# Attention and two feed-forward layers on one core: a new order of the first words (query transposes, row sums, values, weight conversion)

## The chip, the cores and the metric

The kernel runs on one core of one Trainium2 chip. The metric is device time in microseconds (us) of one launch, the median of several runs: 1700.97 us before (three runs, 1700.34 to 1705.41). Engines are named as in the profile: PE (matrix multiply), PEld (its weight loads), DVE (VectorE), ACT (ScalarE), POOL (GpSimd) and SP, whose queue issues most transfers.

## The reference, cut to what matters

```python
B, H, S, D = 8, 8, 576, 64                      # pool = 8, so Sp = 72
k_p = k.reshape(B, H, Sp, 8, D).mean(axis=3)    # v_p the same of v
scores = (1 / sqrt(D)) * q @ k_p.T
attn = exp(scores - scores.max(-1))
attn = attn / (attn.sum(-1) + 1e-9)
x = (attn @ v_p)  # to [4608, 512]
x = (relu(x @ w_in) ** 2) @ w_out               # 512 -> 2048 -> 512
out = leaky(x @ w2_in, 0.01) @ w2_out           # the same sizes
```

The weights come in as 64-bit numbers, two 32-bit words each, and are made into sums of two rounded 32-bit parts (a high and a low one) on the chip.

## The kernel before, in words

The 4608 tokens go in blocks of 512, four tiles of 128 tokens each. The beginning, which the change is about, does four things at once: attention for the four tiles of block 0, then, between the products of the first layer, attention for block 1 (tiles 4 to 7), and all the while the conversion of the first layer's weights, eight pieces of w_in and eight of w_out.

The order is written out by hand. A string, `START`, holds words of a letter and a number; `start()` (line 749) goes through them and issues each word's instructions, and every engine then takes its own in that order, each waiting for its operands. The words:

- `K`, `Q`, `V`, `i`: the loads of keys, of a query tile, of values, of a weight piece (all on SP's queue).
- `k`: pools the keys (DVE, line 429), masks them (446), transposes them on PE (460) and copies them with ACT (464).
- `q`: transposes a query tile on PE (562), and ACT copies it out (567).
- `s`: the scores of a tile on PE (598); for each half DVE takes the maximum (610, "m" below) and ACT four exponentials (619), eight a tile.
- `n`: the row sums (DVE, 630, only where the tile's number is in `early`), their reciprocals and the scaling (631 to 633), and a copy of the last columns (640).
- `P`: the transposes of the probabilities on PE (661, 667) and ACT's two casts (671, 673); `r`: DVE's low parts of them (680).
- `v`: pools the values, matmuls on PE (392) and two sums on DVE (402); `m`: splits them (DVE, 526 to 541); `w`: ACT places them (524, six instructions); `x1`: the key pooling of batch 1 on PE (392).
- `a` to `e` of a weight piece: `a` one ACT pass (231), `b` two DVE passes (235, 238), `c` two (249, 252), `d` one (293), then a cast by ACT (298, `D` on its own) and `e`, one more on DVE (302). In the string before, the word `d` stands for both `d` and the cast.

Behind `start()` come the values of block 0 (PE, lines 712 to 715, with a cast by ACT and a subtraction by DVE for each of four groups), and `first_products()`: 32 units of 12 matmuls each (line 883), the pieces of tiles 4 to 7 and of the conversion hung into them by `second_attention()` and `conversion(u)`. Then `second_products()` (line 921) and the remaining blocks.

PSUM has eight banks: four with the names acc0 to acc3 and four that `bank()` hands out in turn (`ps`). `acc_bank(m)` takes one by name. A new user of a bank waits until the last reader of it is done.

Of the kernel before, what the change touches and what calls it, by code (L numbers as in the profile page):

```python
# [12 lines left out]
AF = mybir.ActivationFunctionType  # L13
ALU = mybir.AluOpType
AX = mybir.AxisListType

P = 128
# [26 lines left out]
def attention_relu2_leaky_kernel(  # L44
# [12 lines left out]
    nc = tc.nc  # L57
    B, H, S, D = q.shape
# [4 lines left out]
    NP = H // 2  # L63
    KEYS = H * SP
    NK = (KEYS + P - 1) // P
    KC = DM // P
    FC = DFF // P
    RD = POOL * D
    RROWS = 6 * REM
    T = 512  # L70
    BLOCKS = NT // T

    START = (
        "K0 Q0 i0 Q1 Q2 Q3 V0 i1 K1 i2 Q4 Q5 i3 "
        "q0 k0 a0 s0 q1 b0 s1 q2 c0 n0 s2 q3 n1 s3 P0 d0 n2 r0 P1 n3 r1 a1 v0 P2 r2 m0 P3 r3 w0 e0 x1"
    ).split()

    common = ctx.enter_context(tc.tile_pool(name="sb", bufs=1, side="left"))
# [64 lines left out]
    def drop(what, b, n):  # L146
        for c in range(n):
            taken((what, b, c))
# [13 lines left out]
    def taken(key):  # L162
        tag = raws.pop(key)[1]
        if tag:
            live[tag] -= 1
            load()
# [58 lines left out]
            for j in range(2)  # L225
        ]

    def exponent(top):


        nc.scalar.activation(out=f32(top), in_=f32(top), func=AF.Copy, scale=2.0**-112)

    def first_bits(val, top):

# [9 lines left out]
            op1=ALU.bitwise_or,  # L244
        )

    def low_term(val, top, low):

        nc.vector.tensor_scalar(
            out=top, in0=val, scalar1=0xFF800000, scalar2=None, op0=ALU.bitwise_and  # L250
        )
        nc.vector.scalar_tensor_tensor(
            out=f32(low),
            in0=low,
            scalar=2.0**-52,
            in1=f32(top),
            op0=ALU.mult,
            op1=ALU.mult,
        )

    def place(kind, i, t):
        for n, to in enumerate(((wih, wil), (woh, wol))[kind]):
# [10 lines left out]
    def weight_steps(w, kind, i):  # L273


        st = {}

        def load_words():
            t = sb([P, 1024, 2], U32, weight_tag(kind, i))
            src, to = words_of(w, kind, i)  # L280
            nc.sync.dma_start(out=to(t), in_=src)
            st["low"], st["top"] = t[:, :, 0], t[:, :, 1]

        def bits():
            val = st["val"] = sb([P, 1024], U32, "val")
            first_bits(val, st["top"])

        def term():
            low_term(st["val"], st["top"], st["low"])

        def high():
            w = st["w"] = f32(st["val"])
            nc.vector.tensor_tensor(out=w, in0=w, in1=f32(st["low"]), op=ALU.add)
            t = st["parts"] = sb([P, 2, 1024], F32R, weight_tag(kind, i))
            place(kind, i, t)

        def high_copy():
            nc.scalar.copy(st["parts"][:, 0], st["w"])

        def low():  # L300
            t = st["parts"]
            nc.vector.tensor_tensor(out=t[:, 1], in0=st["w"], in1=f32(t[:, 0]), op=ALU.subtract)

        return load_words, lambda: exponent(st["top"]), bits, term, high, low, high_copy

    class Weights:

# [71 lines left out]
                self.tick()  # L379


    first_tiles, first_s, early = range(T // P), [], range(2 * T // P)
    kps, kts, kms, vps, vrps, vst, qT, sc = {}, {}, {}, {}, {}, {}, {}, {}
    v_hi = sb([P, NP, P], F32R, "v_hi")
    v_lo = sb([P, NP, P], F32R, "v_lo")
# [90 lines left out]
    def v_pool_pe(b):  # L476

        vps[b] = sb([P, NP, D], F32, "vp")
        vrps[b] = sb([P, 2, D], F32, "vr")
        ps, last = acc_bank(2), acc_bank(3)  # L480
        for cc in range(NP):
            halves(ps, cc, raws[("v", b, cc)][0], P)
        for c in range(2):
            halves(last, c, raws[("rem", b, c)][0], RROWS)
        halves_sum(vps[b], ps, 0, NP)
        halves_sum(vrps[b][:RROWS], last, 0, 2)

    def v_tile_pe(b, what, c):

# [85 lines left out]
    def score_products(i):  # L575

        rest = []
        qt = qT.pop(i)
        if i in first_tiles:
            if not first_s:  # L580
                t = home_tile([P, 3, KEYS]).rearrange("p n (h k) -> p n h k", h=H)
                first_s.extend(t[:, n] for n in range(3))
            s = first_s.pop()
        else:
            s = sb([P, H, SP], F32, "s")
        m = sb([P, H], F32, "m")
        l = sb([P, H], F32, "l")
        for hf in range(2):
            if i in first_tiles:
                ps = acc_bank((2 * i + hf) % KC)  # L590
            else:
                ps = acc_bank(KC - 1) if i in early and hf == 0 else bank()
# [145 lines left out]
    def start():  # L738

        t0, rest = 0, {}  # L740
        for word in START:
            x, n = word[0], int(word[1:])
            if x == "K":
                for c in range(NK):
                    if n:
                        load_to(("k", n, c), k_load(n, c), ("gh", "gl", "gh", "gl", "raw")[c])
                    else:
                        load_home(("k", n, c), k_load(n, c))
                keyed.add(n)
            elif x == "Q":  # L750
                load_q(n)
            elif x == "V":
                for c in range(NP):
                    load_home(("v", n, c), v_load(n, c))
                for c in range(2):
                    load_home(("rem", n, c), rem_load(n, c))
                pooled.add(n)
            elif x == "i":
                w1.load(n)
            elif x in "abcde":  # L760
                w1.do("dD" if x == "d" else x, n)
            elif x == "k":
                for c in range(NK):
                    k_pool(n, c)
                k_mask(n)
                k_transpose(n)
                drop("k", n, NK)
            elif x == "x":
                pooled_late.append(k_pool_pe(n))
                drop("k", n, NK)  # L770
            elif x == "v":
                v_pool_pe(n)
                drop("v", n, NP)
                drop("rem", n, 2)
            elif x == "m":
                v_split(n)
            elif x == "w":
                built.add(n)
                v_place(n)
            elif x == "q":  # L780
                q_transpose(n)
                taken(("q", n))
            elif x == "s":
                scores(n)
            elif x == "n":
                normalize(n)
            elif x == "P":
                rest[n] = p_products(n, 0, t0)
            elif x == "r":
                rest.pop(n)()  # L790
# [201 lines left out]
    w1, w2 = Weights(w1_in, w1_out), Stored(w2_in, w2_out)  # L992
# [62 lines left out]
    LATE, LAST = 6, FC - 3  # L1055
    begins = {2 * n - 2 if n < LATE else 2 * LATE + 1 + (n - LATE) * 5 // 2: n for n in range(1, LAST + 1)}

    def conversion(u):
        if u in begins:
            n = begins[u]  # L1060
            if n < LAST and n + 1 != LATE:
                w1.do("a", n + 1)
            w1.do("bcd" if n == 1 else "cdD", n)
        elif u - 1 in begins:
            n = begins[u - 1]
            if n == 1:
                w1.do("D", n)
            if n < LAST and n + 1 != LATE:
                w1.do("b", n + 1)
            if n != LATE - 1:  # L1070
                w1.do("e", n)
        elif u == 2 * LATE:
            w1.do("ab", LATE)
# [581 lines left out]
```

## Time and profile before

| | us |
|---|---|
| median of the runs (three) | 1700.97 |
| the profiled execution, by itself | 1704.66 |
| its span, first to last instruction | 1702.9 |
| PE busy in the span | 1663.1 |
| DVE, ACT busy | 1156.0, 703.9 |

PE is busy 98% of the span, so its idle stretches are where time can come from. The page's 40 slices are 42.6 us each: PE is at 6 tenths in the first one and at 9 everywhere else but the last. A row of the timeline has the start, the length, the engine, line and operation, out and in, and in brackets the engine's idle time before it and what ended that.

### The profile page before, as it was taken

What the parts mean: (1) busy time and instruction counts of PE and PEld (TensorE: products, weight loads), DVE (VectorE), ACT (ScalarE), POOL (GpSimd) and SP (SyncE); (2) the same over time, 40 slices, a digit from 0 to 9 for tenths busy, and PEclk for the clock granted to TensorE, in tenths of its full rate; (3) what the DMA queues carried; (4) which work ended last, traced back from release to release, by engine and by line L of the source; (5) the groups of instructions that cost most, each with busy time, mean ns of one, the idle gap of its engine ahead of it and who ended that gap; (6) DMA issues with size and microseconds to landing.
All of it is one profiled execution on the core that took longest, in us unless ns stands there. A gap on an engine that the chain in (4) does not pass through costs nothing. (4 is left out here: it accounts for less than half of the span.)

```text
span 1702.9 us, 25369 instructions
## 1 busy us (share of the span) xinstructions
PE 1663.1 (98%) x9608; PEld 1500.0 (88%) x9608; DVE 1156.0 (68%) x2028; ACT 703.9 (41%) x1551; POOL 19.6 (1%) x39
## 2 busy tenths in 40 slices
PE   6999999999999999999999999999999999999998
PEld 5778888888888888888888899999999999999998
DVE  7978886666666667575534677756767866666665
ACT  4545343343443443433433444434444633333332
POOL 0012000000000000000000000000000000000000
PEclk9999999999999999999999999999999999999999
DMA  8924542323233232332001255355437755454443
GB/s 229 342 88 156 173 152 94 89 89 96 88 98 98 86 97 74 96 110 73 30 25 56 86 172 177 118 179 174 170 126 257 259 164 164 150 158 155 155 149 106
DMA packets 197211, 228.24 MB, mean 134 GB/s; under 512 B 49120, under 2 KB 157920, under 8 KB 197088
## 3 DMA queue, kind: packets, MB, share of 16 engines
q1 hardware_dynamic: 193952, 217.70, 39.8%
q0 software_dynamic: 2560, 8.39, 1.3%
q8 instruction: 75, 1.23, 0.3%
q10 hardware_dynamic: 576, 0.52, 0.1%
q14 instruction: 48, 0.39, 0.1%
HBM read 140.58 MB, written 85.98 MB: 133 GB/s over the span
## 5 line engine op out<-in xcount | busy, mean ns | idle before, releaser
L883 PE MATMUL ps<-xh,wi 128*128 128x512 f32 x896 | 296.6, 393 | 0.0
L921 PE MATMUL acc<-gh,wo 128*128 128x512 f32 x1080 | 276.6, 394 | 0.7 <-ACT xl L893 0.7
L921 PEld LDWEIGHTS acc<-gh,wo 128*128 128x128 f32 x1080 | 200.7, 189 | 41.7 <-ACT xl L893 1.2
L883 PEld LDWEIGHTS ps<-xh,wi 128*128 128x128 f32 x896 | 168.2, 188 | 34.6 <-issue 0.2
L883 PE MATMUL ps<-xl,wi 128*128 128x512 f32 x448 | 174.4, 389 | 0.0
L900 DVE CAST gh<-r 128x512 fp32r<-128x512 f32 x112 | 47.6, 425 | 175.0 <-ACT r L896 174.6
L893 ACT ACTIVATE r<-ps 128x512 f32<-128x512 f32 x112 | 67.7, 605 | 207.8 <-PE ps L883 203.6
L921 PE MATMUL acc<-gl,wo 128*128 128x512 f32 x540 | 149.5, 390 | 0.0
L921 PEld LDWEIGHTS acc<-gl,wo 128*128 128x128 f32 x540 | 101.8, 189 | 21.6
L619 ACT ACTIVATE s<-ps,m 128x72 f32<-128x72 f32 x240 | 72.1, 330 | 93.4 <-DVE m L610 93.4
L883 PEld LDWEIGHTS ps<-xl,wi 128*128 128x128 f32 x448 | 84.2, 188 | 16.5
L1537 PE MATMUL acc<-wi,hh 128*128 128x256 f32 x512 | 94.0, 283 | 1.1 <-ACT r L1353 1.1
L1537 PE MATMUL acc<-wo,hh 128*128 128x256 f32 x512 | 93.8, 283 | 0.0
L1537 PE MATMUL ps<-wo,hh 128*128 128x256 f32 x496 | 90.9, 283 | 0.0
L1537 PE MATMUL ps<-wi,hh 128*128 128x256 f32 x496 | 90.9, 283 | 0.0
L1337 PE MATMUL acc<-fh,wi 128*128 128x384 f32 x408 | 88.4, 339 | 1.3 <-DVE gh L1350 0.3
L1337 PE MATMUL ps<-fh,wo 128*128 128x384 f32 x408 | 87.7, 337 | 0.0
L901 DVE TENSOR_TENSOR gl<-r,gh 128x512 fp32r<-128x512 f32 x112 | 77.6, 693 | 7.5
L1537 PEld LDWEIGHTS acc<-wi,hh 128*128 128x128 f32 x512 | 79.9, 192 | 1.3 <-ACT r L1353 1.3
L1537 PEld LDWEIGHTS acc<-wo,hh 128*128 128x128 f32 x512 | 79.9, 192 | 0.0
L1353 ACT ACTIVATE gh<-gh 128x384 f32<-128x384 f32 x48 | 25.3, 526 | 131.1 <-DVE gh L1350 131.1
L1537 PEld LDWEIGHTS ps<-wo,hh 128*128 128x128 f32 x496 | 77.4, 192 | 0.0
(278 smaller groups left out, 3560.9 us busy)
## 6 DMA issues: line engine op xcount, KB each, us to landing
hf<-r SPq DMA_DIRECT2D x96, 192.0 KB
xl<-hf SPq DMA_DIRECT2D x24, 640.0 KB
hr<-hf SPq DMA_DIRECT2D x24, 640.0 KB
xh<-hf SPq DMA_DIRECT2D x23, 640.0 KB
hf<-gl SPq DMA_DIRECT2D x48, 192.0 KB
hf<-gh SPq DMA_DIRECT2D x48, 192.0 KB
hf<-st SPq DMA_DIRECT2D x48, 192.0 KB
wi<-in_moe_w_in SPq DMA_DIRECT2D x8, 1024.0 KB
```

The source lines that it names most:

```text
L619: nc.scalar.activation(out=s[:, g, :], in_=ps[:, h * SP : (h + 1) * SP], func=AF.Exp, bias=m[:, g : g + 1], accum_out=None if i in early e ...
L883: nc.tensor.matmul(ps, lhsT=w[:, kc], rhs=x[kc], start=(kc == 0 and n == 0), stop=(kc == KC - 1 and n == 2),)
L893: nc.scalar.activation(out=r, in_=ps, func=AF.Relu)
L900: nc.vector.tensor_copy(gh, r)
L901: nc.vector.tensor_tensor(out=gl, in0=r, in1=f32(gh), op=ALU.subtract)
L921: nc.tensor.matmul(acc[m], lhsT=w[:, m * P : (m + 1) * P], rhs=x, start=(c == 0 and n == 0), stop=(c == FC - 1 and n == 2),)
L1337: nc.tensor.matmul(at, lhsT=w[:, FORMS[j], kc], rhs=x[j][:, kc], start=m == 0 and j not in (4, 6), stop=m == 5, skip_group_check=True,)
L1353: nc.scalar.activation(out=out_, in_=x, func=AF.Lrelu)
L1537: nc.tensor.matmul(at[:, s * TR : (s + 1) * TR], lhsT=x[:, a, s * P : (s + 1) * P], rhs=w[:, b], start=p == 0 and s == 0 and m == 0, stop= ...
```

## The change

- `START` is ordered anew. Query transposes 1, 2 and 3 come one tile ahead of the scores that need the tile before. Query tiles 0 to 2 are loaded ahead of weight piece 0.
- Weight piece 0's `a b c d` come behind the scores of tile 2, together, instead of being spread from the first scores on; its cast `D` and `e` behind the transposes of tile 1. Piece 1's `b c d` are done before the low parts `r1`, not after the first products have begun.
- `early` is empty: in tiles 0 to 7, too, ACT gives the row sums along with the exponentials, and the row-sum instruction of DVE goes.
- The values are pooled in two of the four turning banks instead of acc2 and acc3, on PE behind the scores of tile 3, and their sums on DVE are a word of their own (`u`).
- `conversion(u)` does the pieces 1 to 4 earlier in the first products. The order of later units stays.
- Engines for the conversion can be chosen by `BY_GPSIMD`, which is empty, so nothing goes to GpSimd.

```diff
+    BY_GPSIMD = ()
     START = (
-        "K0 Q0 i0 Q1 Q2 Q3 V0 i1 K1 i2 Q4 Q5 i3 "
-        "q0 k0 a0 s0 q1 b0 s1 q2 c0 n0 s2 q3 n1 s3 P0 d0 n2 r0 P1 n3 r1 a1 v0 P2 r2 m0 P3 r3 w0 e0 x1"
+        "K0 Q0 Q1 Q2 i0 Q3 V0 i1 K1 i2 Q4 Q5 i3 "
+        "q0 k0 q1 s0 q2 s1 n0 q3 s2 a0 b0 c0 d0 n1 P0 s3 v0 r0 n2 P1 D0 a1 e0 "
+        "n3 u0 P2 m0 b1 c1 d1 r1 P3 w0 r2 x1 r3"
...
-    first_tiles, first_s, early = range(T // P), [], range(2 * T // P)
+    first_tiles, first_s, early = range(T // P), [], range(0)
...
-        ps, last = acc_bank(2), acc_bank(3)
+        ps, last = bank(), bank()
...
-        halves_sum(vps[b], ps, 0, NP)
-        halves_sum(vrps[b][:RROWS], last, 0, 2)
+        def rest():
+            halves_sum(vps[b], ps, 0, NP)
+            halves_sum(vrps[b][:RROWS], last, 0, 2)
+        return rest
...
-            elif x in "abcde":
-                w1.do("dD" if x == "d" else x, n)
+            elif x in "abcdeD":
+                w1.do(x, n)
...
     def conversion(u):
-        if u in begins:
+        if u == 0:
+            w1.do("De", 1)
+            w1.do("abcd", 2)
+        elif u == 1:
+            w1.do("D", 2)
+            w1.do("ab", 3)
+        elif u == 2:
+            w1.do("e", 2)
+            w1.do("c", 3)
+        elif u == 3:
+            w1.do("d", 3)
+        elif u == 4:
+            w1.do("De", 3)
+            w1.do("a", 4)
+        elif u in begins:
```

Three places in the order. The first: DVE from the maxima of tile 0 on, and ACT beside it. `val` and `wi` are of weight piece 0, `m` of the maxima, `l` of the row sums, `wo` holds copies and exponentials of these tiles. DVE before:

```order
L610 TENSOR_REDUCE m<-acc_163 128x4
L610 TENSOR_REDUCE m<-acc_166 128x4
L235 TENSOR_SCALAR val<-wi_95 128x1024
L238 SCALAR_TENSOR_TENSOR val<-wi_95,val 128x1024
L610 TENSOR_REDUCE m<-acc_190 128x4
L610 TENSOR_REDUCE m<-acc_193 128x4
L249 TENSOR_SCALAR wi_95<-val 128x1024
L252 SCALAR_TENSOR_TENSOR wi_95<-wi_95 128x1024
```

and now, from the maxima of tile 2 to those of tile 3:

```order
L624 TENSOR_REDUCE m<-acc_221 128x4
L624 TENSOR_REDUCE m<-acc_224 128x4
L239 TENSOR_SCALAR val<-wi_97 128x1024
L242 SCALAR_TENSOR_TENSOR val<-wi_97,val 128x1024
L253 TENSOR_SCALAR wi_97<-val 128x1024
L257 SCALAR_TENSOR_TENSOR wi_97<-wi_97 128x1024
L303 TENSOR_TENSOR val<-val,wi_97 128x1024
L645 TENSOR_SCALAR l<-l 128x8
L646 RECIPROCAL l<-l 128x8
L647 TENSOR_TENSOR wo_165<-wo_165,l 128x576
L654 COPY prem_82<-wo_165 128x96 x2
L624 TENSOR_REDUCE m<-acc_266 128x4
```

ACT before, from the copy of the keys to the second tile's exponentials:

```order
L469 COPY kt<-ps 128x64
L231 ACTIVATE wi_95<-wi_95 128x1024
L619 ACTIVATE wo_160<-acc_163,m 128x72 x4
L619 ACTIVATE wo_160<-acc_166,m 128x72 x4
L567 COPY wo_145<-ps 128x512
L619 ACTIVATE wo_160<-acc_190,m 128x72 x4
```

and now, from the copy of query tile 3 to the exponentials of tile 3:

```order
L581 COPY wo_145<-ps 128x512
L633 ACTIVATE wo_165,l<-acc_221,m 128x72 x4
L633 ACTIVATE wo_165,l<-acc_224,m 128x72 x4
L233 ACTIVATE wi_97<-wi_97 128x1024
L685 CAST pth<-ps 128x4x128
L687 CAST ptr<-ps 96x2x128
L633 ACTIVATE wo_263,l<-acc_266,m 128x72 x4
```

The pass `a0` (231, now 233) moved on ACT from in front of all exponentials to behind those of three tiles, and all five DVE passes that need it moved in one piece in front of the scaling of tile 1 and the maxima of tile 3.

The second: DVE ahead of the low parts `ptl`, `ptr`. Before, from those of tile 1 on:

```order
L680 TENSOR_TENSOR ptl<-ps,pth 128x4x128
L680 TENSOR_TENSOR ptr<-ps,ptr 32x2x128
L402 TENSOR_REDUCE vp<-acc_314 128x256
L402 TENSOR_REDUCE vr<-acc_315 96x128
L680 TENSOR_TENSOR ptl<-ps,pth 128x4x128
L680 TENSOR_TENSOR ptr<-ps,ptr 32x2x128
L526 TENSOR_SCALAR vh<-vp 128x256
```

and now, from the last row of the split values on:

```order
L555 SCALAR_TENSOR_TENSOR vr<-rh,cst,vr 96x128
L239 TENSOR_SCALAR val<-wi_112 128x1024
L242 SCALAR_TENSOR_TENSOR val<-wi_112,val 128x1024
L253 TENSOR_SCALAR wi_112<-val 128x1024
L257 SCALAR_TENSOR_TENSOR wi_112<-wi_112 128x1024
L303 TENSOR_TENSOR val<-val,wi_112 128x1024
L694 TENSOR_TENSOR ptl<-ps,pth 128x4x128
L694 TENSOR_TENSOR ptr<-ps,ptr 32x2x128
```

The values' sums and split (402, 526 to 541) and the five passes of weight piece 1 now stand ahead of the low parts of tile 1; before, these came ahead of all of them.

The third: PE around the transposes of the probabilities (661 and 667, now 675 and 681), the pooling of the values (392, now 402, from `wo`) and that of the next keys (from `gh` on). Before:

```order
L392 MATMUL acc_315<-wo_104,cst 96x128 x8
L661 MATMUL ps<-cst,wo_160 128x128 x4
L667 MATMUL ps<-cst,prem_81 96x128 x2
L661 MATMUL ps<-cst,wo_250 128x128 x4
L667 MATMUL ps<-cst,prem_82 96x128 x2
L392 MATMUL acc_382<-gh,cst 128x128 x4
```

and now:

```order
L402 MATMUL ps<-wo_104,cst 96x128 x8
L675 MATMUL ps<-cst,wo_165 128x128 x4
L681 MATMUL ps<-cst,prem_82 96x128 x2
L675 MATMUL ps<-cst,wo_165 128x128 x4
L681 MATMUL ps<-cst,prem_81 96x128 x2
L675 MATMUL ps<-cst,wo_263 128x128 x4
L681 MATMUL ps<-cst,prem_82 96x128 x2
L402 MATMUL acc_383<-gh,cst 128x128 x4
```

The pooling of the values writes `ps` instead of acc banks and stands ahead of the transposes of three tiles instead of two; the next keys are still pooled behind the last of them.

## Rows read from the trace of the kernel before

**Rows 1.** The page's first line.

```profile
span 1702.9 us, 25369 instructions
```

**Rows 2.** Stretches: length, busy time of PE, PEld, DVE, ACT, POOL; granted clock, DMA share, GB/s.

```profile
9.50:41.00 31.50, 24.63 (x166) 22.32 (x166) 25.34 (x56) 18.79 (x55) 0.00 (x0) 0.95 0.86 233
45.00:103.00 58.00, 50.64 (x282) 40.69 (x280) 51.87 (x91) 30.51 (x76) 5.99 (x10) 1.00 0.77 278
103.00:169.00 66.00, 65.22 (x279) 53.46 (x280) 54.99 (x60) 35.14 (x50) 12.55 (x22) 0.97 0.35 115
```

**Rows 3.** PE's groups from 9 to 41 us, the scores: count, busy, mean ns, idle before.

```profile
L598 PE MATMUL acc<-kt,wo 128*128 128x144 f32 x32 | 6.5, 360 | 6.8 <-ACT wo L567 6.5 <-ACT kt L464 0.4
```

**Rows 4.** PE in order of time: start, length, what, idle time before and its releaser.

```profile
25.34 1.72 PE L598 MATMUL acc<-kt,wo 128*128 128x144 f32 x8 [3.37 <-ACT wo L567]
...
36.24 1.06 PE L392 MATMUL acc<-gh,cst 128*128 128x128 f32 x8
...
40.92 0.50 PE L712 MATMUL ps<-pth,v_hi 128*128 128x512 f32 x1
...
44.75 0.40 PE L883 MATMUL acc<-xh,wi 128*128 128x512 f32 x1
...
56.02 0.72 PE L883 MATMUL acc<-xh,wi 128*128 128x512 f32 x2 [1.01 <-DVE wi L302]
...
62.53 0.65 PE L598 MATMUL acc<-kt,qt 128*128 128x144 f32 x4
```

**Rows 5.** ACT in order of time: the first tiles, weight piece 2, tile 8 with row sums.

```profile
14.23 1.91 ACT L619 ACTIVATE wo<-acc,m 128x72 f32<-128x72 f32 x8 [0.78 <-DVE m L610]
16.01 0.60 ACT L567 COPY wo<-ps 128x512 f32<-128x512 f32 x1
...
28.42 0.60 ACT L671 CAST pth<-ps 128x512 fp32r<-128x512 f32 x1
...
29.15 1.07 ACT L298 CAST wi<-val 128x1024 fp32r<-128x1024 f32 x1
...
48.98 1.17 ACT L231 ACTIVATE wi<-wi 128x1024 f32<-128x1024 f32 x1
...
182.09 0.31 ACT L619 ACTIVATE s<-ps,m 128x72 f32<-128x72 f32 x1
...
184.46 1.19 ACT L896 ACTIVATE xh<-xh 128x512 f32<-128x512 f32 x2
```

**Rows 6.** DVE in order of time: conversion passes, maxima, scaling, low parts, values.

```profile
15.07 0.68 DVE L235 TENSOR_SCALAR val<-wi 128x1024 uint32<-128x1024 uint32 x1
15.79 1.23 DVE L238 SCALAR_TENSOR_TENSOR val<-wi,val 128x1024 uint32<-128x1024 uint32 x1
...
22.53 0.81 DVE L610 TENSOR_REDUCE m<-acc 128x4 f32<-128x288 f32 x2
...
28.61 0.75 DVE L630 TENSOR_REDUCE l<-wo 128x8 f32<-128x576 f32 x1
29.39 0.17 DVE L631 TENSOR_SCALAR l<-l 128x8 f32<-128x8 f32 x1
...
31.02 0.68 DVE L680 TENSOR_TENSOR ptl<-ps,pth 128x512 fp32r<-128x512 f32 x1
...
35.90 0.69 DVE L402 TENSOR_REDUCE vp<-acc 128x256 f32<-128x512 f32 x1
...
38.12 0.29 DVE L526 TENSOR_SCALAR vh<-vp 128x256 fp32r<-128x256 f32 x1
...
40.06 0.69 DVE L680 TENSOR_TENSOR ptl<-ps,pth 128x512 fp32r<-128x512 f32 x1
...
41.24 1.22 DVE L302 TENSOR_TENSOR wi<-val,wi 128x1024 fp32r<-128x1024 f32 x1
```

**Rows 7.** PE in the first products: a wait for a turning bank (as rows 4).

```profile
70.07 1.16 PE L392 MATMUL ps<-st,cst 128*128 128x128 f32 x8 [0.99 <-DVE ptl L680]
```

**Rows 8.** One stretch behind PE's wait of 3.37 us (columns as in rows 2).

```profile
26.00:27.00 1.00, 1.00 (x6) 0.99 (x6) 0.46 (x1) 0.36 (x2) 0.00 (x0) 0.50 1.06 272
```

More of the change, by code (lines that the diff above doesn't have):

```diff
@@ L226, in half_words_of, with exponent @@
         ]
-    def exponent(top):
-        nc.scalar.activation(out=f32(top), in_=f32(top), func=AF.Copy, scale=2.0**-112)
+    def exponent(top, engine=None):
+        if engine is None:
+            nc.scalar.activation(out=f32(top), in_=f32(top), func=AF.Copy, scale=2.0**-112)
+        else:
+            engine.tensor_scalar(out=f32(top), in0=f32(top), scalar1=2.0**-112, scalar2=None, op0=ALU.mult)
     def first_bits(val, top):
@@ L245, in first_bits, with low_term @@
         )
-    def low_term(val, top, low):
+    def low_term(val, top, low, engine=None):
+        engine = engine or nc.vector
         nc.vector.tensor_scalar(
@@ L251, in low_term @@
         )
[L252 to L259, printed above, removed]
+        if engine is nc.vector:
+            engine.scalar_tensor_tensor(
+                out=f32(low),
+                in0=low,
+                scalar=2.0**-52,
+                in1=f32(top),
+                op0=ALU.mult,
+                op1=ALU.mult,
+            )
+        else:
+            engine.tensor_scalar(out=f32(low), in0=low, scalar1=2.0**-52, scalar2=None, op0=ALU.mult)
+            engine.tensor_tensor(out=f32(low), in0=f32(low), in1=f32(top), op=ALU.mult)
     def place(kind, i, t):
@@ L276, in weight_steps @@
         st = {}
+        by = nc.gpsimd if kind == 0 and i in BY_GPSIMD else None
+        engine = by or nc.vector
         def load_words():
@@ L288, in term @@
         def term():
-            low_term(st["val"], st["top"], st["low"])
+            low_term(st["val"], st["top"], st["low"], by)
         def high():
             w = st["w"] = f32(st["val"])
-            nc.vector.tensor_tensor(out=w, in0=w, in1=f32(st["low"]), op=ALU.add)
+            engine.tensor_tensor(out=w, in0=w, in1=f32(st["low"]), op=ALU.add)
             t = st["parts"] = sb([P, 2, 1024], F32R, weight_tag(kind, i))
@@ L301, in low @@
             t = st["parts"]
-            nc.vector.tensor_tensor(out=t[:, 1], in0=st["w"], in1=f32(t[:, 0]), op=ALU.subtract)
-        return load_words, lambda: exponent(st["top"]), bits, term, high, low, high_copy
+            engine.tensor_tensor(out=t[:, 1], in0=st["w"], in1=f32(t[:, 0]), op=ALU.subtract)
+        return load_words, lambda: exponent(st["top"], by), bits, term, high, low, high_copy
     class Weights:
@@ L591, in score_products @@
             else:
-                ps = acc_bank(KC - 1) if i in early and hf == 0 else bank()
+                ps = acc_bank(KC - 1) if i < 2 * T // P and hf == 0 else bank()
             for b, _, r0, n in reversed(parts_of(i)):
@@ L771, in start @@
             elif x == "v":
-                v_pool_pe(n)
+                sums = v_pool_pe(n)
                 drop("v", n, NP)
                 drop("rem", n, 2)
+            elif x == "u":
+                sums()
             elif x == "m":
@@ L1062, in conversion @@
                 w1.do("a", n + 1)
-            w1.do("bcd" if n == 1 else "cdD", n)
+            if n > 3:
+                w1.do("cdD", n)
         elif u - 1 in begins:
             n = begins[u - 1]
-            if n == 1:
-                w1.do("D", n)
             if n < LAST and n + 1 != LATE:
                 w1.do("b", n + 1)
-            if n != LATE - 1:
+            if n not in (3, LATE - 1):
                 w1.do("e", n)
```

## The prediction

> **What bounds the kernel now.** I read the page first: the profiled execution has a span of 1702.9 us [rows 1]. PE is busy nearly all through, so only the beginning has time to give. Next the stretches. From 9.5 to 41 us PE is idle for 31.5 - 24.63 = 6.9 us; from 45 to 103 for 58 - 50.64 = 7.4; from 103 to 169 for 0.8. The granted clock costs (1 - 0.95) x 31.5 = 1.6 us in the first stretch and (1 - 0.97) x 66 = 2.0 in the third [rows 2]. DVE is busy 25.34 of 31.5 us in the first and 51.87 of 58 in the second: there DVE, not PE, sets the pace, and PE's gaps are places where it waits for DVE or for ACT. The groups say what ends PE's gaps among the scores: 6.8 us before the scores, 6.5 of them until ACT has copied a query tile [rows 3]. The change aims at this wait. But what ends the stretch is not the scores: the values begin at 40.92 right behind the pooling of the next keys, which began at 36.24, and DVE's last low part runs from 40.06 to 41.24 [rows 4, 6]. PE and DVE arrive together. So whether the scores come sooner matters only if DVE's own chain gets shorter.
>
> **The first term: when the values begin.** I follow ACT and DVE through their new order; each takes its own in the order written.
>
> ACT. The first exponentials start at 14.23 [rows 5]; four more transposes ahead of the first scores make that 14.5. A tile's eight exponentials took 16.01 - 14.23 = 1.78 us without row sums, and 184.46 - 182.09 = 2.37 in tile 8, which has them: 0.59 more a tile [rows 5]. A query copy is 0.60, 0.5 from start to start. Three tiles and two copies: 14.5 + 3 x 2.37 + 2 x 0.5 = 22.6. Only then comes `a0`, 1.17 by the same pass of a later piece [rows 5]: 23.8. Before, it was done before the first exponentials.
>
> DVE. It has the maxima of three tiles and one scaling behind it at about 20, and its next instruction needs `a0`. It stands idle for some 3.8 us, with the scaling of tile 1 and the maxima of tile 3 queued behind. From 23.8: `b0` is 0.68 + 1.23, `c0` the same two kinds of pass, `d0` 1.22 as the pass at 41.24; with 0.04 between dependent ones 5.2 [rows 6]: 29.0. Scaling of tile 1, from 29.39 to 31.02 without its row sum, 1.6: 30.6. Maxima of tile 3, 0.8: 31.4; ACT starts that tile's exponentials on the first half, at 31.0, and ends them at 33.4, then the casts of tile 1 (29.15 - 28.42 = 0.7) and the cast `D0` (1.07): 35.2 [rows 5]. DVE meanwhile: low parts of tile 0 (41.24 - 40.06, about 1.1) 32.5; scaling of tile 2 34.1; then it waits for `D0` to 35.2; `e0` 36.4; scaling of tile 3 38.0; the values' sums (35.90 to 38.12 less the 1.1 of a low part, 1.0) 39.0; their split (40.06 - 38.12 = 1.9) 40.9; `b1 c1 d1`, 5.2, 46.1; low parts of tile 1, 47.2 [rows 6].
>
> PE. Its transposes of tile 3 go to the banks that tile 1's low parts are still read from: four turning banks hold two tiles' worth, and the values' pooling now takes two of them as well. So they start at 47.2. The pooling of the next keys, 40.92 - 36.24 = 4.7 for 40 matmuls [rows 4], stands behind them: with six transposes at the same 0.12 each, 52.6. PE has then been idle for most of 15 us. After its wait of 3.37 us the granted clock was 0.50, the 1.2 GHz level [rows 4, 8]; such a stretch costs 0 here if it ends in time and 1.6 if it does not; I take the middle, 0.8. The values begin at 53.4 instead of 40.92: **12.5 us late**.
>
> What the change takes away lies inside this: 6.8 us of PE's waits and 4 x (29.39 - 28.61 = 0.78) = 3.1 us of DVE's row sums [rows 3, 6] are gone, but DVE has got 5.2 + 1.2 us more to do before the values and 3.8 + 1.1 us of waits. Bounds: without any low clock 11.7; with `a0` a microsecond later and a full low stretch 14.3.
>
> A rule that bears on the bank: PE waited 0.99 us at 70.07 to reuse a turning bank that DVE had not yet read [rows 7]; turning banks don't hide an evacuation that is late in DVE's queue. The Trainium skill, Perfetto Trace Analysis, section Optimizing Tensor Performance, says that independent matmul groups should rotate through PSUM banks so that the evacuation of one overlaps the next group's matmuls; if rotation alone did that, tile 3 would not be held, and its case stands among the rivals below.
>
> **The second term: the first products, from there to the second products.** PE's own work is the same. Before, this stage has 7.4 + 0.8 us of idle time and 2.0 of clock, 10.2 in all [rows 2]: it can give back at most that. For giving back: DVE has done `b1 c1 d1` (5.2) already and is rid of four row sums (3.1). Against: ACT pays 4 x 0.59 = 2.4 more, and pieces 2 and 3 are now made in the first units, with ACT's cast `D` and pass `a` each waiting on DVE and DVE on them, ahead of the relus, exponentials and query copies. I walk the first place. Products begin 3.83 after the values, as before (44.75 - 40.92): 57.2. `a2` began at 48.98, 4.2 behind the first product [rows 4, 5]; now `D1` stands there at 61.4 and `a2` behind it: 63.5. `b2 c2 d2` 68.8, `D2` 69.9, `a3` 71.0, `b3` 73.0, maxima of tile 4 73.8, its exponentials 75.8, relu and query copy 76.9. PE comes to the scores that need this copy 62.53 - 44.75 = 17.8 behind the first product, 16.8 without the 1.01 it waited for a weight there [rows 4], so at 74.0: it waits 2.9. Carried on in the same way, an estimate from the same rows, the queues leave PE idle for 10.4 us in the stage in place of 8.2, and the clock is low after two more waits (1.6 each): +5.4. I take **+5**. Bounds: -10.2 (nothing is ever waited for) and +10 (twice the waits).
>
> Moves with no price. Query tiles 1 and 2 pass weight piece 0 on SP's queue: the piece lands later by two query tiles, but `a0` now comes 10 us later than it did; tile 1 must land one transfer behind tile 0. The later loads on SP's queue (queries 6 and 7, values and weights) wait for PE's key pooling and move with it by some 12 us, as do their users. POOL's stores follow the relus. The pooling of the values stands on PE ahead of tile 1's transposes, which wait for DVE until 32 anyway; if its last rows landed later than that, PE would wait, and nothing else before 47.
>
> **Sum.** 12.5 + 5 = +17.5 us. Against the profiled execution by itself, 1704.66, that is 1722.2; against the median of the runs, 1700.97, which lies 3.7 lower, **1718.5**.
>
> **The rivals.**
> 1. The stage gives back (chance 0.12). DVE enters the products 8.3 us lighter, and PE's waits there shrink by 3 to 10 us: 12.5 - 10 to 12.5 - 3, 1703.5 to 1710.5. For: DVE is busy 89% of that stage before. Against: what PE waits for in my walk is ACT's order, not DVE's load.
> 2. The banks don't hold tile 3 (0.08). Then its transposes follow its scaling at 38, the keys are pooled by 44, and the last low part, 47.2 + 2 x 1.1 = 49.4, decides: values at 49.4, +8.5, with the stage +13.5: 1714.5. For: nothing in the trace of before shows a tile's transposes held for long. Against: the wait at 70.07 is of just this kind.
> 3. Faster (0.03). DVE's order isn't felt: neither `b1 c1 d1` (5.2) nor the waits for `a0` and `D0` (4.9) nor the key pooling behind tile 3's transposes (6.2) lies on the path. That is 16.3 off 53.4: values at 37.1, 3.8 early; with half of the stage's 10.2 won too, 1692. It decides if `a0` is done by 20, when DVE asks for it. Against: three tiles of exponentials stand in front of it on ACT, 7.1 us by themselves.
> 4. No change (0.03): the second rival's first term and the first rival's stage together, about 1701.
>
> On row sums the rows show a fair trade, 0.59 on ACT for 0.78 on DVE. The Trainium skill, ScalarE: Activation LUTs, section Rules for kernel authors, would leave adds on VectorE; by that `a0` would end 1.8 sooner and three scalings on the chain would take 2.3 longer, so the sum would be 0.5 more.
>
> **How the numbers follow.** The forecast has 0.74, its own range being 1712.5 (first term 11.7, stage 0) to 1724 (14.3 and 9). The range for 8 in 10 reaches down into the first rival, 1708, and up to 1724; it leaves out the faster case, no change, the lower part of the first rival and a little at the top. A measurement of this kernel can tell 0.3%, 5.1 us, from no change. Faster 0.03; within 0.3% the fourth case and the lowest quarter of the first, 0.06; slower 0.91.
>
> **What would show it.** Right: DVE idle 3 to 4 us at about 20 until ACT's line 233; the exponentials of tile 3 only at about 31; PE idle before each tile's transposes (line 675) with DVE as releaser, the longest of 5 us or more; values at 52 to 55; a wait of 2 to 3 us for ACT at the scores of tile 5; second products 15 to 19 us later than before. The second term alone is wrong if the values are that late and the second products are not. The whole is wrong if the values begin before 45, which would mean that DVE did not stand behind `a0`.

## The result, and the profile after

The changed kernel takes 1723.17 us (median of four runs, 1722.80 to 1723.87), the kernel before, timed beside it, 1703.05 (four runs, 1700.34 to 1705.41): a ratio of 1.0113, 95% interval 1.0100 to 1.0126. The profiled execution of the changed kernel takes 1722.8 by itself and has this span, on its page:

```profile
span 1721.0 us, 25428 instructions
```

That is 18.1 us more than in [rows 1]. The stretches of the changed kernel, cut where its stages now lie (length, busy time of PE, PEld, DVE, ACT and POOL, granted clock, DMA share, GB/s):

```profile
9.50:41.00 31.50, 19.41 (x119) 16.93 (x117) 20.31 (x47) 18.07 (x79) 0.00 (x0) 0.79 0.82 235
41.00:53.40 12.40, 6.96 (x39) 6.85 (x40) 7.80 (x11) 3.04 (x8) 0.00 (x0) 0.57 0.06 24
58.10:185.00 126.90, 115.41 (x552) 94.02 (x551) 97.46 (x137) 66.15 (x154) 17.53 (x31) 0.97 0.52 183
```

The first row stands against the first of [rows 2]: in the same 31.5 us PE does 19.41 us of work instead of 24.63, DVE 20.31 instead of 25.34, and the granted clock is 0.79 instead of 0.95. Both engines wait for each other and for ACT. The third row runs from the first products to the second. For the kernel before, the same cut is

```profile
44.70:167.00 122.30, 114.16 (x552) 92.76 (x552) 105.23 (x146) 63.70 (x123) 18.14 (x32) 0.99 0.54 191
```

so that this stage is 4.6 us longer, 3.4 of it PE's idle time (126.9 - 115.41 = 11.5 against 122.3 - 114.16 = 8.1) and 1.2 busy time at a lower granted clock (0.97 against 0.99). DVE has 7.8 us less to do there and PE still waits longer.

The wait that the change aims at is gone from the group that answers to [rows 3], 1.0 us of idle time where it was 6.8:

```profile
L612 PE MATMUL acc<-kt,wo 128*128 128x144 f32 x32 | 5.8, 332 | 1.0 <-ACT wo L581 1.0
```

What came in its place stands in PE's timeline of the changed kernel, in order of time, [rows 4] before:

```profile
28.67 1.99 PE L402 MATMUL ps<-wo,cst 96*96 96x128 f32 x8 [3.07 <-DMA raw<-in_k]
31.58 1.09 PE L675 MATMUL ps<-cst,wo 128*128 128x128 f32 x4 [0.92 <-DVE ptl L694]
38.58 1.09 PE L675 MATMUL ps<-cst,wo 128*128 128x128 f32 x4 [5.49 <-DVE vp L412]
46.44 1.08 PE L675 MATMUL ps<-cst,wo 128*128 128x128 f32 x4 [6.34 <-DVE ptl L694]
47.74 1.91 PE L402 MATMUL acc<-gh,cst 128*128 128x128 f32 x8
...
52.34 1.06 PE L402 MATMUL acc<-gl,cst 128*128 128x128 f32 x8
...
54.34 0.50 PE L726 MATMUL ps<-pth,v_hi 128*128 128x512 f32 x1
...
58.17 0.40 PE L899 MATMUL acc<-xh,wi 128*128 128x512 f32 x1
...
77.96 0.76 PE L612 MATMUL acc<-kt,qt 128*128 128x144 f32 x4 [2.63 <-ACT qt L581]
88.25 1.16 PE L402 MATMUL ps<-st,cst 128*128 128x128 f32 x8 [2.69 <-ACT s L633]
...
184.70 2.11 PE L937 MATMUL acc<-gh,wo 128*128 128x512 f32 x8 [0.74 <-ACT xl L909]
```

The transposes of tiles 2 and 3 (line 675, the third and fourth row) wait 5.49 and 6.34 us for DVE, those of tile 2 for the sums of the values, which are read from the turning banks, and those of tile 3 for the low parts of tile 1. The pooling of the next keys runs its first pieces at 1.91 us each, where one took 1.06 in [rows 4]; the granted clock is 0.50 in the row around them:

```profile
45.00:49.00 4.00, 2.56 (x12) 2.57 (x13) 3.62 (x7) 1.44 (x4) 0.00 (x0) 0.50 0.00 0
```

The values begin at 54.34 instead of 40.92: 13.4 us late. The second products (line 937) begin at 184.70; in the kernel before at 166.51:

```profile
166.51 2.11 PE L921 MATMUL acc<-gh,wo 128*128 128x512 f32 x8 [0.74 <-ACT xl L893]
```

That is 18.2 us, and from there to the end the changed kernel takes 1536.3 and the kernel before 1536.4. All of the loss is made in the first 185 us. DVE's and ACT's timelines of the changed kernel say why DVE is late, the [rows 5, 6] of before:

```profile
23.35 0.69 DVE L239 TENSOR_SCALAR val<-wi 128x1024 uint32<-128x1024 uint32 x1 [4.47 <-ACT wi L233]
...
34.86 1.23 DVE L312 TENSOR_TENSOR wi<-val,wi 128x1024 fp32r<-128x1024 f32 x1 [1.29 <-ACT wi L308]
...
40.50 0.68 DVE L239 TENSOR_SCALAR val<-wi 128x1024 uint32<-128x1024 uint32 x1
...
45.61 0.68 DVE L694 TENSOR_TENSOR ptl<-ps,pth 128x512 fp32r<-128x512 f32 x1
```
```profile
22.02 1.30 ACT L233 ACTIVATE wi<-wi 128x1024 f32<-128x1024 f32 x1
...
30.57 0.32 ACT L633 ACTIVATE wo<-acc,m 128x72 f32<-128x72 f32 x1 [6.59 <-DVE m L624]
```

`b0` waits 4.47 us for `a0`, which ACT starts only at 22.02; the maxima of tile 3 stand behind `b0 c0 d0`, so ACT in turn waits 6.59 us for them; `e0` waits 1.29 for the cast `D0`; and from 40.50 to 45.61 piece 1 stands ahead of the low parts of tile 1, which PE waits for.

### The profile page after: what moved, and what is told of

Read it like the earlier page. It is cut to its first block, busy times and chain, and to the rows that moved or that the text cites. A ratio compares the mean times of both kernels' runs of the same rounds, so it can differ in the third digit from the quotient of the medians.

```text
span 1721.0 us, 25428 instructions
## 1 busy us (share of the span) xinstructions
PE 1666.6 (97%) x9608; PEld 1502.9 (87%) x9608; DVE 1150.2 (67%) x2020; ACT 709.1 (41%) x1615; POOL 19.1 (1%) x39
```

## The experiments

Theory: the first term is DVE's chain, lengthened by its wait for `a0`, by `e0` and by piece 1 ahead of `r1`, and handed on to PE by the turning banks and by the key pooling behind the last transposes; the second term is the earlier conversion in the first products. By the code these are the last steps of piece 1 and the pieces 2 and 3; piece 4 keeps its units, though the list of the change names it too. The main rivals: the row sums or the query order cost by themselves, or PE's own order decides. In the table every column but the last is from the profiled execution; "stage" is from the values to the second products, "idle" is PE's idle time from the first products to the second. The last column is the ratio to the kernel before, timed beside each, with its 95% interval. From the second products to the end these traces take 1534.7 to 1539.9 us, so the starts are better evidence than the ratios for steps of 1 or 2 us.

| kernel | values begin | second products | stage | idle | ratio |
|---|---|---|---|---|---|
| before | 40.92 | 166.51 | 125.59 | 8.1 | 1 |
| changed | 54.34 | 184.70 | 130.36 | 11.5 | 1.0113 [1.0100, 1.0126] |
| a0 early | 50.39 | 180.76 | 130.37 | 11.5 | 1.0092 [1.0077, 1.0107] |
| r1 first | 49.21 | 178.43 | 129.22 | 10.6 | 1.0090 [1.0075, 1.0105] |
| keys early | 50.33 | 183.75 | 133.42 | 10.5 | 1.0104 [1.0087, 1.0120] |
| no piece 1 | 48.61 | 173.46 | 124.85 | 7.7 | 1.0053 [1.0038, 1.0068] |
| row sums alone | 42.39 | 166.66 | 124.27 | 8.7 | 1.0003 [0.9994, 1.0011] |
| queries alone | 40.81 | 164.86 | 124.05 | 8.1 | 0.9991 [0.9982, 0.9999] |
| own banks | 60.35 | 191.25 | 130.90 | 10.6 | 1.0151 [1.0138, 1.0164] |
| new order A | 40.29 | 162.41 | 122.12 | 6.9 | 0.9980 [0.9969, 0.9992] |
| table back | 53.70 | 176.67 | 122.97 | 7.7 | 1.0077 [1.0062, 1.0093] |
| three back | 41.81 | 166.65 | 124.84 | 7.7 | 1.0012 [1.0003, 1.0022] |
| new order B | 39.45 | 162.28 | 122.83 | 6.8 | 0.9985 [0.9974, 0.9995] |
| kept parts | 40.77 | 164.37 | 123.60 | 6.7 | 0.9991 [0.9981, 1.0001] |

**a0 early** (changed kernel, one word moved).

```diff
-q0 k0 q1 s0 q2 s1 n0 q3 s2 a0 b0 c0 d0 ...
+q0 k0 q1 s0 a0 q2 s1 n0 q3 s2 b0 c0 d0 ...
```

> The changed kernel with one word moved: a0 (ScalarE's first pass over weight piece 0) stands behind the exponentials of tile 0 instead of behind those of tile 2. Theory (VectorE's chain sets when the values begin, and a0 is at its head): in the changed kernel VectorE's b0 starts at 23.35 us after an idle time of 4.47; here a0 is done before VectorE asks for it, b0 starts at about 20, everything behind it on VectorE comes 3.4 earlier, the values begin at 51 instead of 54.34, and the time is 3 to 4 us below the changed kernel's, 1719 to 1720. If the values are held by something else (PE's banks or its own order), the idle time goes and the values stay at 54: no difference.

DVE's timeline of this kernel:

```profile
18.57 0.95 DVE L623 TENSOR_REDUCE m<-acc 128x4 f32<-128x288 f32 x2 [0.64 <-PE acc L611]
19.44 0.68 DVE L238 TENSOR_SCALAR val<-wi 128x1024 uint32<-128x1024 uint32 x1
```

`b0` follows the maxima of tile 2 without a wait, 3.91 us earlier than in the changed kernel; the values come 3.95 earlier, the second products 3.94. What `b0` gained went through to the second products in full. The ratios give 3.6 us (0.0021 of 1704); their intervals overlap, the traces' steps agree to 0.04.

**r1 first.**

```diff
-... P2 m0 b1 c1 d1 r1 P3 ...
+... P2 m0 r1 b1 c1 d1 P3 ...
```

> The changed kernel with r1 (VectorE's low parts of tile 1) ahead of b1 c1 d1 (five passes over weight piece 1) instead of behind them. Theory (four turning banks: PE's transposes of tile 3 wait for the last reader of tile 1's banks): they start at about 41.6 instead of 46.44, the pooling of the next keys behind them moves by as much, and the values begin at 49.5, when VectorE's last low parts and ScalarE's placing are also done: 5 us below the changed kernel, about 1718; up to 7 if the low clock in the key pooling goes as well. Rival (the banks do not hold tile 3; VectorE's last low parts decide, since b1 c1 d1 are still ahead of them): values at 53 or later, no difference over 1 us.

PE's timeline of this kernel:

```profile
40.95 1.09 PE L674 MATMUL ps<-cst,wo 128*128 128x128 f32 x4 [1.23 <-DVE ptl L693]
```

The low parts of tile 1 start at 40.12 here, and the transposes of tile 3 follow 0.83 us behind that start, the same distance as in the changed kernel (45.61 and 46.44): it is those low parts, through the banks, that hold them, as expected. The values come 5.1 us earlier, the second products 6.3. The time gains less, 3.9 us by the ratios. Some 1.5 of the 2.4 us between the two lie in the next block: one wait there, 1.6 us in both traces, was followed by a longer stretch of low clock here. What is left lies within the intervals of the ratios. One row each, from 50 to 100 us behind the start of the second products, of the changed kernel and of this one:

```profile
234.70:284.70 50.00, 48.35 (x240) 40.87 (x239) 39.48 (x88) 21.08 (x78) 0.00 (x0) 0.97 0.38 118
```
```profile
228.43:278.43 50.00, 48.38 (x234) 40.87 (x233) 39.46 (x88) 21.07 (x78) 0.00 (x0) 0.94 0.38 117
```

**keys early.**

```diff
-... n3 u0 P2 ... r2 x1 r3
+... n3 u0 x1 P2 ... r2 r3
```

> The changed kernel with the pooling of the next keys on PE (x1) ahead of the transposes of tile 2 instead of behind those of tile 3. It fills a stretch in which PE waits. Theory: PE's order costs what stands between tile 3's transposes (46.44) and the values (54.34); with the key pooling gone from there the values begin when VectorE's r3 and ScalarE's placing of the values are done, at about 50: 4 us below the changed kernel, about 1719. Rival (VectorE alone decides, PE's order does not matter): values at 54, no difference.

The values begin 4.0 us earlier, as expected, but the second products only 0.95: the idle time that the key pooling filled is now right ahead of the values, and they pay for it. PE's timeline of this kernel, and the stretch of the values:

```profile
47.50 1.09 PE L674 MATMUL ps<-cst,wo 128*128 128x128 f32 x4 [7.01 <-DVE ptl L693]
...
52.57 0.63 PE L725 MATMUL ps<-pth,v_hi 128*128 128x512 f32 x1
```
```profile
50.30:56.90 6.60, 6.57 (x17) 4.88 (x18) 1.62 (x4) 3.12 (x7) 0.00 (x0) 0.58 0.30 93
```

A matmul of the values takes 0.63 us instead of 0.40 at a granted clock of 0.58, and the values take 6.53 us (50.33 to the first products at 56.86) instead of 3.83. The expectation missed the time by that.

**no piece 1.** Taken back: `b1 c1 d1` among the first words, and `conversion(u)`.

```diff
-... P2 m0 b1 c1 d1 r1 P3 ...
+... P2 m0 r1 P3 ...
     def conversion(u):
-        if u == 0:
-            w1.do("De", 1)
-            w1.do("abcd", 2)
...
-        elif u in begins:
+        if u in begins:
```

> The changed kernel without the part that does weight piece 1 early: b1 c1 d1 are out of the first words and done behind the start of the first products, and the pieces 1 to 4 are converted in the units in which the kernel before converts them. Theory: VectorE is rid of 5.2 us ahead of r1, so the values begin at about 48 (6.4 earlier than 54.34), and the stage from the first products to the second products is again as long as before (121.8 instead of 126.5): 10 to 11 us below the changed kernel, about 1712 to 1713, still 10 above the kernel before. Rival (work done early is given back later): values at 48, but the stage is longer by those 5.2 us than in the changed kernel: 1722, no difference over 2 us.

Values 5.7 earlier, stage 5.5 shorter, the time about 10 us below the changed kernel (1.0113 to 1.0053). Two things are taken back at once here, so the two terms are not yet told apart. But taking the work out did not make the stage longer: the rival falls.

**table back.** Only `conversion(u)` is taken back; the first words stay.

> The changed kernel with conversion(u) as in the kernel before, apart from b c d of piece 1, which are done among the first words as in the changed kernel: the pieces 2 to 4 are made in the units in which the kernel before makes them. The first words are those of the changed kernel. Theory (the second term comes from the earlier units of the conversion, through ScalarE's order): the values begin at 54.34 as in the changed kernel, from there to the second products it takes 120 to 126 us instead of 130.4, and the time is 5 to 10 below the changed kernel, 1713 to 1718. Rival (the stage is longer because ScalarE gives the row sums of tiles 4 to 7): the stage stays at 130, no difference over 2 us.

The stage is 122.97 us, 7.4 shorter than in the changed kernel, with the same row sums by ScalarE. So the second term lies in the units in which the conversion is done. The stretch of the first products, of this kernel and of no piece 1, which differ only in where `b1 c1 d1` stand:

```profile
57.60:177.00 119.40, 111.72 (x551) 91.45 (x550) 97.35 (x137) 66.15 (x154) 17.60 (x31) 1.00 0.55 195
```
```profile
52.40:173.80 121.40, 113.75 (x552) 92.53 (x551) 102.12 (x142) 66.32 (x154) 17.55 (x31) 0.99 0.54 193
```

PE is idle for 7.7 us in both, where the changed kernel has 11.5 and the kernel before 8.1. DVE has 4.8 us less to do in this kernel and PE waits no less. Against the changed kernel 3.8 us of the 7.4 are idle time and 3.6 busy time at a higher granted clock (1.00 against 0.97). The stage is also 2.6 us shorter than before, but 2.2 of these are the clock (1.00 against 0.99). How much of the clock belongs to the order, and how much to the one execution that was traced, is not shown. Ahead of the values, piece 1 costs 5.1 us (53.70 against 48.61). The values begin 0.6 us earlier than in the changed kernel although nothing ahead of them was altered: the key pooling left the low clock sooner, its third group of eight matmuls taking 1.06 us instead of 1.35.

Of PE's waits in the changed kernel at 77.96 and 88.25 none is left, the scores of tile 5 run at 74.03 without one; the nearest in this kernel's timeline are

```profile
80.64 1.16 PE L402 MATMUL ps<-st,cst 128*128 128x128 f32 x8 [0.75 <-DVE ptl L694]
85.49 0.76 PE L612 MATMUL acc<-kt,qt 128*128 128x144 f32 x4 [0.96 <-ACT qt L581]
```

In the changed kernel the wait at 77.96 comes to PE through both queues. In ACT's timeline there, the cast `D2` waits for DVE's passes over piece 2, and the exponentials of tile 4 for its maxima, which stand behind DVE's `b3`, which waits for ACT's `a3`:

```profile
69.87 1.05 ACT L308 CAST wi<-val 128x1024 fp32r<-128x1024 f32 x1 [4.40 <-DVE val L303]
...
74.41 0.32 ACT L633 ACTIVATE s<-acc,m 128x72 f32<-128x72 f32 x1 [1.98 <-DVE m L624]
```

**row sums alone** (kernel before): `early` empty, with line 592's bank still taken by the tile's number.

```diff
-    first_tiles, first_s, early = range(T // P), [], range(2 * T // P)
+    first_tiles, first_s, early = range(T // P), [], range(0)
```

> The kernel before with one part of the change: the row sums of tiles 0 to 7 come from ScalarE along with the exponentials, and VectorE's row-sum instructions go. Theory: 0.59 us a tile more on ScalarE against 0.78 less on VectorE, and before the values neither decides by itself: the values stay within 1 us of 40.92, the time within 2 us of the kernel before. Rival (VectorE's load alone sets the pace): eight times 0.78 saved, values 2 to 3 us earlier and the time 3 to 6 below. Other rival (ScalarE's length counts): values 2.4 later, the time 2.5 to 5 above.

No difference in the time. The values begin 1.5 us later, half a microsecond more than the theory allowed. Two things are longer in this trace: a tile's exponentials on ACT, by 0.59 us, and the scores on PE, 467 ns a matmul instead of 360:

```profile
L598 PE MATMUL acc<-kt,wo 128*128 128x144 f32 x32 | 9.2, 467 | 5.7 <-ACT wo L567 5.3 <-ACT kt L464 0.4
```

In the old order a tile's exponentials, the next copy, transpose and scores follow each other in turn, so both are felt there; how the 1.5 us divide between them is not shown. The stage is 1.3 shorter, but PE's idle time in it is not (8.7 us against 8.1): the gain is the granted clock, 1.00 instead of 0.99.

**queries alone** (kernel before, with the changed kernel's order of loads, too).

```diff
-q0 k0 a0 s0 q1 b0 s1 q2 c0 n0 s2 q3 n1 s3 ...
+q0 k0 q1 s0 a0 q2 s1 b0 q3 c0 n0 s2 n1 s3 ...
```

> The kernel before with one part of the change: query transposes 1 to 3 and their copies one tile ahead of the scores that need the tile before, query tiles 0 to 2 loaded ahead of weight piece 0; a0 moves behind the exponentials of tile 0, as its piece now lands later, and the other conversion words stay between the tiles. Theory (VectorE's chain sets when the values begin): PE's 6.8 us of waits ahead of the scores nearly all go, the values do not move (within 1 us of 40.92), and the time is within 2 us of the kernel before. Rival (PE's waits at the scores were on the path, the change took them away and lost by other parts): values 4 to 7 us earlier, the time 4 to 7 below the kernel before.

PE's group of the scores in this kernel:

```profile
L598 PE MATMUL acc<-kt,wo 128*128 128x144 f32 x32 | 5.4, 318 | 2.1 <-ACT wo L567 2.1
```

4.7 of the 6.8 us of waits are gone and the values begin at 40.81, 0.1 us earlier. The wait that the change aims at was not on the path. The stage is 1.5 us shorter with the same idle time of 8.1 us. The ratio, 0.9991 [0.9982, 0.9999], is barely below 1.

**own banks** (changed kernel).

```diff
-        ps, last = bank(), bank()
+        ps, last = acc_bank(2), acc_bank(3)
```

> The changed kernel with the values pooled into acc2 and acc3 again instead of two turning banks. Theory: acc2 and acc3 hold the scores of the first tiles, the pooling stands on PE behind the scores of tile 3 and must wait until tile 3's exponentials have read their bank, 33.0 in the changed kernel instead of 21; its 48 matmuls (6 us) and behind them the transposes of tile 1 come later by some 6, and the time is 5 to 8 us above the changed kernel, about 1729. Rival (the turning banks taken by the values are what holds the transposes of tiles 2 and 3): with them free again the transposes come sooner, and the time is 3 to 6 us below the changed kernel.

Values 6.0 later, 1.0151: in the new order the turning banks for the values are a gain. PE's timeline:

```profile
32.32 7.36 PE L402 MATMUL acc<-wo,cst 128*128 128x128 f32 x48 [10.81 <-ACT wo L633]
...
53.56 1.09 PE L675 MATMUL ps<-cst,wo 128*128 128x128 f32 x4 [12.57 <-DVE ptl L694]
```

**three back** (changed kernel): `a0` behind `s0`, no piece 1 among the first words with `conversion(u)` as before, `e0` behind `r2`.

> The changed kernel with three things undone at once: a0 stands behind the exponentials of tile 0, piece 1 is not begun ahead of the first products (conversion(u) as in the kernel before), and e0 stands behind the low parts of tile 2 instead of ahead of the scaling of tile 3, where VectorE waited 1.29 us for ScalarE. Query order, row sums by ScalarE, values in turning banks stay as in the changed kernel. Theory: 3.4, 5.7 and some 2.5 come off 54.34, so the values begin at 41 to 43, the stage is as long as before, and the time is within 3 us of the kernel before, 1702 to 1707. Rival (one of the parts that stay costs by itself): 1710 or more.

1705.89 us, ratio 1.0012 [1.0003, 1.0022], values at 41.81. These three places make up 12.5 of the 13.4 us and, with the table, the whole of the stage's loss. The place of `e0` was not moved by itself: if the three add up, a0 early and no piece 1, 4.0 and 5.7 us, leave some 2.9 us for it. What stays of the change costs some 2 us together, by the interval 0.5 to 3.7.

**new order A, new order B, kept parts.** Three tries for something faster than both. A and B keep query order, row sums and turning banks, and order the rest anew, the conversion in the first units of the first products, too; B also loads as the kernel before does. The lines below show only the words behind the loads. Kept parts is the kernel before with the query order and the row sums of above and `b1` moved in front of `e0`.

```diff
+q0 k0 q1 s0 q2 s1 n0 a0 q3 s2 n1 P0 s3 b0 r0 P1 c0 n2 r1 v0 d0 D0 n3 a1 P3 u0 m0 P2 x1 r2 w0 r3 b1 e0
```
```diff
+q0 k0 q1 s0 q2 s1 a0 q3 s2 n0 n1 P0 b0 r0 s3 P1 c0 v0 n2 d0 P2 D0 a1 u0 n3 m0 r1 x1 e0 w0 r2 P3 r3 b1
```
```diff
+q0 k0 q1 s0 a0 q2 s1 b0 q3 c0 n0 s2 n1 s3 P0 d0 n2 r0 P1 n3 r1 a1 v0 P2 r2 m0 P3 r3 w0 b1 e0 x1
```

> The parts of the change that the theory finds harmless (query transposes ahead, row sums by ScalarE, values in turning banks) with the words in another order: a0 behind the exponentials of tile 1, the maxima of tile 3 ahead of b0, c0 and d0 apart, r0 and r1 early, piece 1 not begun on VectorE ahead of the low parts, the transposes of tile 3 ahead of those of tile 2, the key pooling ahead of the last steps; and the units of the first products take the pieces 1 to 4 one step later. Theory: none of the waits of the changed kernel is left (b0 not held by ScalarE, no tile's transposes held for over 3 us), the values begin at about 39 to 40, and the time is 3 to 6 us below the kernel before, 1696 to 1701. If what costs in the change is the row sums or the query order itself, it stays above the kernel before by 3 us or more.

> Another order with the same parts (query transposes ahead, row sums by ScalarE, values in turning banks): loads as in the kernel before, a0 behind the exponentials of tile 1, b0 c0 d0 apart from each other, the transposes of tile 2 right behind VectorE's d0 and the key pooling ahead of those of tile 3, c and d of piece 1 in unit 1. Theory: VectorE waits nowhere over 1 us from the maxima of tile 1 on, the values begin at 38 to 40 and the time is 4 to 8 us below the kernel before, 1696 to 1700. Rival (what was won before the values is given back in the first products): values at 39, the time within 2 us of the kernel before.

> The kernel before with three parts of the change alone: query transposes 1 to 3 one tile ahead (as in the run that had this part alone), row sums of tiles 0 to 7 by ScalarE, and of piece 1 only b1 done early, on VectorE behind the values' last low parts and ahead of e0, where no tile's transposes wait for it. The units of the first products keep their pieces. Theory (what the change has to give lies in the first products: in the kernel before PE waits 1.01 us there for a weight part of piece 1, and more behind it): the values begin within 1 us of 40.9, the stage from there to the second products takes 122 to 123 us instead of 125.6, and the time is 2 to 5 us below the kernel before, 1699 to 1702. Rival (b1 ahead of e0 and of the values' own low parts holds the first products): the first products begin 1.9 later, no difference over 2 us.

A is faster than both kernels: 1700.49 us, 0.9980 [0.9969, 0.9992], about 3.4 us below the kernel before. B gives 0.9985 [0.9974, 0.9995], less than expected for its values at 39.45; kept parts, 0.9991 [0.9981, 1.0001], can't be told from the kernel before, where 2 to 5 us and a stage of at most 123 were expected. The intervals of these three and of queries alone overlap, so which of them is fastest is not shown. In A the values come only 0.6 us earlier; 3.5 us are won in the stage behind them, 1.2 of them PE's idle time (6.9 us against 8.1) and the rest busy time at a higher granted clock (1.00 against 0.99). In these orders the time ahead of the values gave little.

## Why the prediction was right, step by step

Against the profiled execution the forecast was 1722.2 us; that of the changed kernel took 1722.8. Against the median it was 1718.5, and 1723.17 was measured, 4.7 us more. Of these, 2.1 are the base: the median of three runs was 1700.97, over the four beside the changed kernel it is 1703.05. The other 2.6 are that these medians lie 20.1 us apart where the sum said 17.5; the profiled executions lie 18.1 apart. The mechanism was right; that the sum came so near is in part luck, since its errors have opposite signs in both terms.

- *Scores.* The waits went, as said, and nothing came of it: queries alone shows that they cost 0.1 us before the values.
- *The wait for `a0`.* Forecast 3.8 us, measured 4.47, of which a0 early got 3.9 back. DVE was ready at 18.9, not 20, and `a0` was done at about 23.3, not 23.8.
- *DVE's chain.* `b0 c0 d0` 5.1 us (forecast 5.2), tile 3's exponentials at 30.57 (31.0), `e0` at 34.86 (35.2), `b1 c1 d1` 5.1 (5.2), transposes of tile 3 at 46.44 (47.2). None of these is off by more than 0.8.
- *The banks.* The second rival, that they don't hold tile 3, is refuted by r1 first: the transposes move with the low parts. Turning banks alone did not decouple them, as the wait in [rows 7] let one suspect. The Trainium skill (Perfetto Trace Analysis, Optimizing Tensor Performance) asks for rotation so that the evacuation of one group overlaps the next group's matmuls. The tiles did rotate here, and PE still waited 6.34 us, since the evacuation stood behind other work in DVE's queue.
- *The low clock.* This is the mis-sized term: 0.8 us taken, 0 to 1.6 as bounds. From the transposes of tile 3 to the values it took 54.34 - 46.44 = 7.9 us, where the durations of before give 5.4: 2.5 us, outside the bounds. PE waited not once but four times between 25 and 46 us, and worked at the low level through the transposes and more than half of the key pooling. So the values came at 54.34, not 53.4: 1.7 us too little here, 0.8 too much in the chain before.
- *The values' rows.* The prediction left out the load of the last value rows, as harmless unless they land after 32. PE did wait 3.07 us for them, to 28.67, and it was harmless, since the next transposes waited for DVE until 31.58 in any case.
- *The stage.* +5 forecast, 130.36 - 125.59 = +4.8 measured. The wait at the scores of tile 5 was 2.63 (2.9 forecast). That the sum fits is partly luck, for the split was off: idle time rose by 3.4, not 2.2, with a second wait of 2.69 for ACT's exponentials at 88.25 that the walk did not reach, and the lower clock cost 1.2, not 3.2.
- *The first rival*, that the stage gives back because DVE has less to do, got the wrong price even where the table of before is kept: with piece 1 done early PE is idle for 7.7 us (table back), without it for 7.7 (no piece 1), and for 8.1 in the kernel before. It wanted 3 to 10 us less. The prediction's argument against it, that PE's waits there are not set by DVE's load, held; its opening sentence, that DVE, busy 51.87 of 58 us, sets the pace there, did not.
- *Row sums.* A fair trade, as the rows said: 1.0003 for this part alone. The Trainium skill, ScalarE: Activation LUTs (Rules for kernel authors), puts adds on VectorE; whether it means sums given along with an activation it does not say, and in the time of this kernel it makes no difference. The 0.5 us that the prediction drew from it is too small to be seen here.

## What to carry to other kernels

Before removing a wait, look at what ends the stretch in which it lies: PE's 6.8 us among the scores were slack beside DVE's chain, and taking most of them away alone moved the values by 0.1 us. When work is moved in an in-order queue, list what it now stands in front of: here `a0` behind three tiles' exponentials, and piece 1 in front of low parts that a PSUM bank and so PE's transposes waited for, cost about 4 and 5 us. Doing work early pays only if it ends a wait later on: `b1 c1 d1` done early cost 5.1 us before the values and took nothing off PE's idle time behind them, 7.7 us with and without it, so DVE's load did not set that time.

## What the runs showed of the hardware

- Where PE's idle time lies decides which work runs at the low clock. In the changed kernel it was the key pooling (1.91 us a piece instead of 1.06, at a granted clock of 0.50, the 1.2 GHz level), in keys early the values (0.63 instead of 0.40 at a granted clock of 0.58). Moving work into the idle time moved the cost: of 4.0 us won ahead of the values, 2.7 were lost in them.
- The same wait of 1.6 us in the next block was followed by a mean granted clock of 0.97 over 50 us in the changed kernel and a0 early, and of 0.94 in r1 first, keys early and no piece 1. That is 1.5 us (0.03 of 50), while DVE and ACT do the same work in that stretch to 0.1 us. Why one wait is followed by the longer stretch is not shown. Differences of that size between two of these kernels say nothing about their order.
- The row sums on ACT are instructions of their own. One group of ACT's from 9 to 41 us in the changed kernel:

```profile
L633 ACT ACTIVATION_READ_ACCUMULATOR wo<-acc,m 128x1 f32 x32 | 8.1, 260 | 0.0
```

They overlap the exponentials in the trace, and a tile's eight exponentials take 0.59 us longer with them.
